# Selectors out of the identity, a new bank plan for the opening, and another order of loads in a fused attention and feed-forward kernel

## Chip, cores and metric

One NeuronCore of one Trainium2 chip. The metric is the device time of one execution in microseconds (us). A profile's span is about 1.8 us shorter than the time of its own run. Every run told here was at a mean granted TensorE clock of 0.99 to 1.0.

## The reference

The kernel takes float32 inputs: q, k, v of shape (8, 8, 576, 64), w_in (512, 2048), w_out (2048, 512). It gives (4608, 512) in float32. Cut to what matters:

```python
def phi(x):
    return np.where(x > 0, x, np.exp(x) - 1.0) + 1.0
q_p, k_p = phi(q), phi(k)
kv  = einsum('bhsd,bhse->bhde', k_p, v)
z   = sum(k_p, axis=2)
num = einsum('bhsd,bhde->bhse', q_p, kv)
den = einsum('bhsd,bhd->bhs', q_p, z)[..., None] + 1e-06
attn = num / den
x = attn.transpose(0, 2, 1, 3).reshape(4608, 512)
h = x @ w_in
out = (h - np.tanh(h)) @ w_out
```

## The kernel before

The feed-forward part is 9 chunks of 512 tokens, each of 64 dense 128x512 matmuls with w_in (16 column blocks `fi` by 4 pairs of heads `p`) and 64 with w_out. They run on TensorE one after the other. The attention of the 8 batches (576 tokens each) is threaded between them: lists `s1[fi]` and `s2[s]` say after which of the 16 w_in blocks, or after which of the 16 w_out steps, a piece of attention is put into the instruction streams. The kernel uses PSUM as one tile, `ps_all`, of eight banks of 128 x 512 float32.

To divide by the denominator, its reciprocal (it lies in four groups of 32 partitions, one for each quarter of the tokens, with a row per head) has to be spread over 128 partitions. Batches 0 and 1 do this on TensorE, by a matmul with a 0/1 matrix, the selector ("spread"), and then multiply on VectorE ("scale"). The later batches write the reciprocals to DRAM (`ds`) and read them back with a broadcast (`rdb`).

The parts that matter here; `...` marks a cut, the comments are mine, and the conditions on the chunk are worked out:

```python
s8 = const.tile([128, 3, NP, 2], F32, name="s8")
...
load_q(0)
make_identity(nc, ident)                  # POOL
load_k(0)
load_v(0)

nc.gpsimd.memset(s8, 0.0)                 # the selectors: 12 selects on POOL
for n in range(3):
    for t in range(4):
        r = slice(32 * t, 32 * t + 32)
        nc.gpsimd.affine_select(out=s8[r, n], in_=s8[r, n], compare_op=ALU.not_equal, fill=1.0,
            base=-8 * n, channel_multiplier=1, pattern=[[-1, NP], [-4, 2]])
for g in range(4):
    load_wi(g)                            # all loads are issued by POOL, in this order
load_k(1)
load_wo(0)
load_q(1)
load_wo(1)
load_v(1)
load_wo(2)
load_wo(3)
...
# opening: attention of batch 0
a_den(0, Banks([0]))
ns0 = new_ns(0)
b0_num(0, ns0, 1)                         # numerators in banks 4, 5; ACT copies them to ns0
b0_kv(1)
bp_a = a_spread_pe(0, 0, (0, 2))          # spread in banks 0 to 3
b0_kz(1)
b0_num(1, ns0, 6)
bp_b = a_spread_pe(0, 4, (1, 3))          # spread in banks 4 to 7
for n, p in enumerate((0, 2, 1, 3)):
    a_scale(0, p, ns0, (bp_a, bp_b)[n // 2], 144 * (n % 2))
...
# chunk 0: where the attention of batch 1 stands
s1[13].append(lambda: a_kphi(1, 0))
s1[15].append(lambda: a_kphi(1, 1))
s2[1].append(lambda: a_qphi(1, 0))
s2[3].append(lambda: a_qphi(1, 1))
s2[5].append(lambda: a_qT_pe(1, 0, side))
s2[6].append(lambda: a_qT_pe(1, 1, side))
s2[7].append(lambda: a_kv(1, side))
s2[9].append(lambda: (a_den(1, side), a_split(1)))
s2[10].append(num1)
s2[12].append(lambda: spread1(0))
s2[13].append(lambda: a_qphi(2, 0))
s2[14].append(lambda: spread1(1))
s2[15].append(lambda: (a_qphi(2, 1), a_qT_dma(2)))
...
# chunk 1: batch 2, and the loads of batch 3
s1[7].append(lambda: a_kv(2, attn))
s1[10].append(lambda: (a_den(2, attn), a_spread(2)))
for p in range(NP + 1):
    s2[9 + p].append(lambda p=p: a_num(2, p))
s1[1].append(lambda: a_kphi(2, 0))
s1[3].append(lambda: a_kphi(2, 1))
s1[0].append(lambda: (gate(gT, 0), load_k(3), load_q(3), load_v(3)))
```

## Time and profile before

| | |
|---|---|
| time, median of 3 runs | 303.54 us (303.45 to 303.79) |
| span of the profiled run (303.01 us) | 301.2 us |
| first product of k of batch 0 (opening) | 12.38 us |
| first w_in matmul of chunk 0 | 20.25 us |
| first w_out matmul of chunk 0 ("B") | 34.07 us |
| first w_in matmul of chunk 2 ("D") | 87.72 us |

The last four rows are starts on TensorE. From D to the end every kernel of this study takes 213.4 to 213.8 us, so a kernel is told by three lengths: the start of the first product of k, from there to B, and B to D. The page, the waits and the opening are shown in the prediction. One more view is worth having, the chain that ended last (start, us, what). In its first 40 us it goes, after k of batch 0, through two transfers of weights:

```profile
14.21 8.53 DMA w_in_sb<-in_moe_w_in_dram
23.03 15.81 DMA w_out_sb<-in_moe_w_out_dram
38.88 1.89 PE ps_all L333 x8
```

The second block of w_out arrives at 38.84 us, and the matmul that needs it starts at 38.88.

### The profile page before, as it was taken

What the parts mean: (1) busy time and instruction counts of PE and PEld (TensorE: products, weight loads), DVE (VectorE), ACT (ScalarE), POOL (GpSimd) and SP (SyncE); (2) the same over time, 40 slices, a digit from 0 to 9 for tenths busy, and PEclk for the clock granted to TensorE, in tenths of its full rate; (3) what the DMA queues carried; (4) which work ended last, traced back from release to release, by engine and by line L of the source; (5) the groups of instructions that cost most, each with busy time, mean ns of one, the idle gap of its engine ahead of it and who ended that gap; (6) DMA issues with size and microseconds to landing.
All of it is one profiled execution on the core that took longest, in us unless ns stands there. A gap on an engine that the chain in (4) does not pass through costs nothing.

```text
span 301.2 us, 4766 instructions
## 1 busy us (share of the span) xinstructions
PE 288.7 (96%) x1804; PEld 137.2 (46%) x1804; DVE 181.9 (60%) x313; ACT 149.6 (50%) x229; POOL 52.9 (18%) x100
## 2 busy tenths in 40 slices
PE   8869989899989999999999999999999999999994
PEld 2534454354445444544454445444544444444443
DVE  4779836898457854785578656865682458008600
ACT  3627824865625652566256625662562166127411
POOL 8963351060006000600060005100000000000000
PEclk9999999999999999999999999999999999999999
DMA  7899999988969776878788876977108310131032
GB/s 104 135 181 207 201 206 206 218 127 145 219 142 144 127 188 138 151 122 191 150 135 139 192 150 89 185 173 167 38 2 192 73 35 0 37 70 35 2 70 70
DMA packets 38902, 38.82 MB, mean 129 GB/s; under 512 B 16800, under 2 KB 33632, under 8 KB 38112
## 3 DMA queue, kind: packets, MB, share of 16 engines
q0 software_dynamic: 17600, 18.35, 38.2%
q1 hardware_dynamic: 21280, 20.17, 29.9%
q8 instruction: 14, 0.23, 0.3%
q14 instruction: 8, 0.07, 0.1%
HBM read 43.78 MB, written 9.55 MB: 177 GB/s over the span
## 4 chain that ended last, share of the span: by engine, by line
PE 79%; DMA 14%; DVE 2%; POOL 2%; ACT 1%; issue 1%; SPq 0%; DVEq 0%; ACTq 0%; POOLq 0%
PE ps_all L318 35%; PE ps_all L333 35%; DMA w_out_sb<-in_moe_w_out_dram 5%; PE ps_all L174 4%; DMA w_in_sb<-in_moe_w_in_dram 3%; DMA rdb<-ds 3%; PE ps_all L269 2%; DMA kraw<-in_k_dram 2%; DMA ds<-rden 1%; PE ps_all L515 1%; POOL qraw L88 1%; ACT e L131 1%; PE ps_all L226 1%; POOL kraw L88 1%; DVE xT L311 0%
## 5 line engine op out<-in xcount | busy, mean ns | idle before, releaser
L318 PE MATMUL ps_all<-xT,w_in_sb 128*128 128x512 bf16 x576 | 128.2, 379 | 2.4 <-DMA w_in_sb<-in_moe_w_in_dram 1.4
L333 PE MATMUL ps_all<-w_out_sb,gT 128*128 128x512 bf16 x560 | 128.3, 379 | 1.2 <-DMA w_out_sb<-in_moe_w_out_dram 1.2
L324 DVE TENSOR_TENSOR gT<-ps_all,th 128x512 bf16<-128x512 f32 x144 | 97.1, 688 | 51.0 <-ACT th L323 50.3
L323 ACT ACTIVATE th<-ps_all 128x512 f32<-128x512 f32 x144 | 85.2, 598 | 53.0 <-PE ps_all L318 48.0
L318 PEld LDWEIGHTS <-w_in_sb 128*128 128x128 bf16 x576 | 55.3, 98 | 69.5 <-issue 2.5
L333 PEld LDWEIGHTS <-gT 128*128 128x128 bf16 x560 | 54.0, 98 | 66.7 <-issue 3.3
L339 ACT COPY osb<-ps_all 128x512 f32<-128x512 f32 (+1 forms) x37 | 21.2, 574 | 78.4 <-PE ps_all L333 58.7
L280 DVE TENSOR_TENSOR xT<-ps_all,rdb 128x512 bf16<-128x512 f32 x24 | 16.3, 690 | 14.2 <-PE ps_all L269 12.1
L107 POOL DMA_DIRECT2D v<-in_v_dram x32 | 19.3, 644 | 8.5 <-DMA w_in_sb<-in_moe_w_in_dram 3.6
L131 ACT ACTIVATE e<-qraw 128x1152 bf16<-128x1152 bf16 x16 | 18.5, 1161 | 4.0 <-DMA qraw<-in_q_dram 4.0
L329 POOL COPY g<-gT 1x1 bf16<-1x1 bf16 x5 | 0.9, 177 | 109.7 <-DVE gT L324 109.7
L133 DVE TENSOR_TENSOR kp<-e,r 128x1152 bf16<-128x1152 bf16 x16 | 12.1, 758 | 12.1 <-ACT e L131 11.1
L131 ACT ACTIVATE e<-kraw 128x1152 bf16<-128x1152 bf16 x16 | 18.6, 1163 | 0.5 <-DMA kraw<-in_k_dram 0.5
L133 DVE TENSOR_TENSOR qp<-e,r 128x1152 bf16<-128x1152 bf16 x16 | 12.1, 758 | 8.1 <-ACT e L131 7.4
L174 PE MATMUL ps_all<-v,kp 64*128 64x192 bf16 x252 | 11.6, 243 | 0.0
L269 PE MATMUL ps_all<-qT,kz 128*128 128x512 bf16 x28 | 10.1, 379 | 1.4 <-DVE xT L280 1.4
L174 PEld LDWEIGHTS <-kp 64*128 64x128 bf16 x252 | 10.0, 94 | 3.0 <-issue 2.5
L390 PE MATMUL ps_all<-zero 128*128 128x512 bf16 x32 | 9.4, 455 | 1.2 <-DVE zero L346 1.2
L92 POOL DMA_DIRECT2D kraw<-in_k_dram x14 | 8.7, 635 | 6.6 <-ACT th L323 3.9
L92 POOL DMA_DIRECT2D qraw<-in_q_dram x14 | 8.8, 640 | 5.7 <-DVE qp L133 4.3
L132 DVE TENSOR_SCALAR r<-qraw 128x1152 bf16<-128x1152 bf16 x16 | 7.4, 464 | 2.3 <-DMA qraw<-in_q_dram 2.3
L183 DVE TENSOR_TENSOR kz<-ps_all,mask 128x320 bf16<-128x320 f32 x14 | 6.2, 485 | 3.4 <-PE ps_all L174 3.4
(72 smaller groups left out, 98.4 us busy)
## 6 DMA issues: line engine op xcount, KB each, us to landing
out_dram<-osb SPq DMA_DIRECT2D x70, 128.0 KB
rdb<-ds SPq DMA_DIRECT2D x12, 576.0 KB
v<-in_v_dram POOLq DMA_DIRECT2D x32, 144.0 KB, 7.9
kraw<-in_k_dram POOLq DMA_DIRECT2D x14, 288.0 KB, 5.0
qraw<-in_q_dram POOLq DMA_DIRECT2D x14, 288.0 KB, 7.3
w_in_sb<-in_moe_w_in_dram POOLq DMA_DIRECT2D x4, 512.0 KB, 9.5
w_out_sb<-in_moe_w_out_dram POOLq DMA_DIRECT2D x4, 512.0 KB, 13.7
qraw<-in_q_dram POOLq DMA_DIRECT2D x4, 144.0 KB, 3.8
```

What stands on the lines that cost most here:

```text
L92: nc.gpsimd.dma_start(out=t[64 * hg:64 * hg + 64].rearrange("p i h j d -> p (i h) (j d)"), in_=src[b, 4 * hg:4 * hg + 4].rearrange("h (p j ...
L107: nc.gpsimd.dma_start(out=v_b[b % 2][64 * hg:64 * hg + 64, i, 0:2].rearrange("p h j d -> p h (j d)"), in_=v[b, h0:h0 + 2].rearrange("h (p ...
L131: return (lambda: nc.scalar.activation(e, x, AF.Exp), lambda: nc.vector.tensor_scalar(r, x, 0.0, 1.0, ALU.max, ALU.add), lambda: nc.vector ...
L133: lambda: nc.vector.tensor_tensor(y, e, r, ALU.min))
L174: nc.tensor.matmul(ps[hg], kp[r, i, j].rearrange("p h d -> p (h d)"), vt[r, i, :, j, :], start=(j == 0), stop=(j == J - 1))
L269: nc.tensor.matmul(ps, kz[:, p // 2, p % 2, 0:128], qT[:, p % 2, 0:8, p // 2, :], start=True, stop=True)
L280: nc.vector.tensor_mul(xT[:, p, S * b:S * b + 512].rearrange("p (j t c) -> p j t c", j=8, t=4), ps.rearrange("p j (t c) -> p j t c", t=4), ...
L318: nc.tensor.matmul(h, w_in_sb[:, p, fi * 128:(fi + 1) * 128], xT[:, p, c * 512:(c + 1) * 512], start=(n == 0), stop=(n == NP - 1))
L323: nc.scalar.activation(th, h, AF.Tanh)
L324: nc.vector.tensor_sub(gT[:, fi, :], h, th)
L333: nc.tensor.matmul(o, gT[:, fi, i * 128:(i + 1) * 128], w_out_sb[:, fi, :], start=(fi == 0), stop=(fi == NF - 1))
L339: nc.scalar.copy(osb[:, f0:f1], o[:, f0:f1])
```

## The change

Its intent has four parts. (1) The selectors are cut out of the identity matrix by four small ACT copies and four DVE copies, so POOL issues w_in 4 us earlier. (2) The opening's spreads move to banks 4 to 7 so that w_in matmuls can start in banks 0 and 1 while the scales still run, with the last 64 tokens of batch 0 scaled by way of DRAM. (3) The second and third blocks of w_out are loaded ahead of q and v of batch 1. (4) The attention of chunks 0 and 1 is placed at other steps to fit. The core of the diff; `[...]` marks a cut, and the comments in added lines are mine:

```diff
-    s8 = const.tile([128, 3, NP, 2], F32, name="s8")
+    s8 = const.tile([128, 3, 2, NP], F32, name="s8")
[...]
-    nc.gpsimd.memset(s8, 0.0)
-    for n in range(3):
-        for t in range(4):
-            r = slice(32 * t, 32 * t + 32)
-            nc.gpsimd.affine_select(
-                out=s8[r, n], in_=s8[r, n], compare_op=ALU.not_equal, fill=1.0, base=-8 * n,
-                channel_multiplier=1, pattern=[[-1, NP], [-4, 2]])
     for g in range(4):
         load_wi(g)
     load_k(1)
     load_wo(0)
+    load_wo(1)
     load_q(1)
-    load_wo(1)
+    load_wo(2)
     load_v(1)
-    load_wo(2)
     load_wo(3)
[...]
+    for t in range(4):
+        nc.scalar.copy(s8[32 * t:32 * t + 32, 0].rearrange("q h p -> q (h p)"),
+                       ident[32 * t:32 * t + 32, 32 * t:32 * t + 8])
[...]
-    b0_num(0, ns0, 1)
+    b0_num(0, ns0)                 # now in banks 1 to 3
     b0_kv(1)
-    bp_a = a_spread_pe(0, 0, (0, 2))
     b0_kz(1)
-    b0_num(1, ns0, 6)
-    bp_b = a_spread_pe(0, 4, (1, 3))
-    for n, p in enumerate((0, 2, 1, 3)):
-        a_scale(0, p, ns0, (bp_a, bp_b)[n // 2], 144 * (n % 2))
+    b0_rest()                      # last 64 tokens: reciprocals to DRAM and back
+    b0_spread((0, 2), 0)           # banks 4 to 7, first 512 tokens
+    b0_scale(0, ns0, 0)
+    b0_scale(2, ns0, 1)
+    b0_num(1, ns0)
+    b0_spread((1, 3), 2)           # banks 4 to 7 again, other columns
+    b0_scale(1, ns0, 2)
+    b0_scale(3, ns0, 3)
[...]
-            s1[13].append(lambda: a_kphi(1, 0))
[...]
+            s1[6].append(lambda: b0_scale_rest(ns0))
+            s1[12].append(lambda: a_kphi(1, 0))
+            s1[14].append(lambda: a_kphi(1, 1))
+            s2[3].append(lambda: a_qphi(1, 0))
+            s2[5].append(lambda: a_qphi(1, 1))
+            s2[6].append(lambda: a_qT_pe(1, 0, side))
+            s2[7].append(lambda: a_qT_pe(1, 1, side))
+            s2[10].append(lambda: a_kv(1, side))
+            s2[12].append(lambda: (a_den(1, side), num1(), a_split(1)))
+            s2[14].append(lambda: spread1(0))
+            s2[15].append(lambda: (spread1(1), a_qphi(2, 0), a_qphi(2, 1), a_qT_dma(2)))
         elif n1 < B:
-            s1[7 if c == 1 else 5].append(lambda: a_kv(n1, attn))
-            s1[10 if c == 1 else 8].append(lambda: (a_den(n1, attn), a_spread(n1)))
+            s1[8 if c == 1 else 5].append(lambda: a_kv(n1, attn))
+            s1[11 if c == 1 else 8].append(lambda: (a_den(n1, attn), a_spread(n1)))
             for p in range(NP + 1):
-                s2[9 + p].append(lambda p=p: a_num(n1, p))
+                s2[(11 if c == 1 else 9) + p].append(lambda p=p: a_num(n1, p))
         if c == 1:
-            s1[1].append(lambda: a_kphi(2, 0))
-            s1[3].append(lambda: a_kphi(2, 1))
+            s1[4].append(lambda: a_kphi(2, 0))
+            s1[5].append(lambda: a_kphi(2, 1))
[...]
         if c == 0:
-            for n, p in enumerate((0, 2, 1, 3)):
-                for fi in range(4):
-                    l1mm(c, fi, hs[fi], p, n)
+            order = [(0, 0), (0, 1), (2, 0), (2, 1), (0, 2), (0, 3), (2, 2), (2, 3)]
+            order += [(p, fi) for p in (1, 3) for fi in range(4)]
+        elif c == 1:
+            hs = [dense() for fi in range(4)]
+            order = [(p, fi) for p in range(NP) for fi in range(4)]
[...]
```

In chunk 1 the first four blocks of w_in now go pair by pair, and their tanh, subtraction and attention pieces come after all sixteen matmuls. Cut from this excerpt is a small fifth piece: exp and minimum of the second half of k of batch 0 are done in two instructions each instead of one.

More of the change, by code (lines that the diff above doesn't have):

```diff
@@ L121, with phi_pieces @@
     kp_t, qp_t, qT_t, kz_t, rdb_t, rden_t = {}, {}, {}, {}, {}, {}
-    def phi_pieces(b, src, store, name, i):
+    def phi_pieces(b, src, store, name, i, parts=0):
         if i == 0:
@@ L130, in phi_pieces @@
         y = store[b][:, i].rearrange("p j h d -> p h j d")
+        if parts:
+            return ([lambda h=h: nc.scalar.activation(e[:, h], x[:, h], AF.Exp) for h in range(2)],
+                    lambda: nc.vector.tensor_scalar(r, x, 0.0, 1.0, ALU.max, ALU.add),
+                    [lambda h=h: nc.vector.tensor_tensor(y[:, h], e[:, h], r[:, h], ALU.min) for h in range(2)])
         return (lambda: nc.scalar.activation(e, x, AF.Exp),
@@ L206, in b0_kz, with b0_num @@
         nc.vector.tensor_mul(kz_t[0][:, :, i, 0:128], ps_all[:, 4 + 2 * i:6 + 2 * i, 0:128], mask[:, :, i, 0:128])
-    def b0_num(i, ns, rem):
+    def b0_num(i, ns):
         kz, qT = kz_t[0], qT_t[0]
         for hg in range(2):
-            nc.tensor.matmul(ps_all[:, rem, 64 * hg:64 * hg + 64], kz[:, hg, i, 0:128], qT[:, i, 8, hg, :],
+            nc.tensor.matmul(ps_all[:, 1, 64 * hg:64 * hg + 64], kz[:, hg, i, 0:128], qT[:, i, 8, hg, :],
                              start=True, stop=True)
@@ L214, in b0_num @@
         for hg in range(2):
-            nc.tensor.matmul(ps_all[:, 4 + hg, :].rearrange("p (j t) -> p j t", j=8), kz[:, hg, i, 0:128],
+            nc.tensor.matmul(ps_all[:, 2 + hg, :].rearrange("p (j t) -> p j t", j=8), kz[:, hg, i, 0:128],
                              qT[:, i, 0:8, hg, :], start=True, stop=True)
-        nc.scalar.copy(ns[:, i::2, 8, :], ps_all[:, rem, 0:128].rearrange("p (a t) -> p a t", a=2))
-        nc.scalar.copy(ns[:, i::2, 0:8, :].rearrange("p a j t -> p a (j t)"), ps_all[:, 4:6, :])
+        nc.scalar.copy(ns[:, i::2, 8, :], ps_all[:, 1, 0:128].rearrange("p (a t) -> p a t", a=2))
@@ new lines, in b0_num, with b0_spread, b0_scale @@
+        nc.scalar.copy(ns[:, i::2, 0:8, :].rearrange("p a j t -> p a (j t)"), ps_all[:, 2:4, :])
+    def b0_spread(pairs, n0):
+        for n, p in enumerate(pairs):
+            for t in range(4):
+                r = slice(32 * t, 32 * t + 32)
+                nc.tensor.matmul(ps_all[:, 4 + t, 128 * (n0 + n):128 * (n0 + n) + 128],
+                                 sel[r, p].rearrange("p h e -> p (h e)"), rden_t[0][r, 0:128], start=True, stop=True)
+    def b0_scale(p, ns, n):
+        nc.vector.tensor_mul(
+            xT[:, p, 0:512].rearrange("p (j t c) -> p t j c", j=8, t=4),
+            ns[:, p, 0:8].rearrange("p j (t c) -> p t j c", t=4),
+            ps_all[:, 4:8, 128 * n:128 * n + 128].rearrange("p t (j c) -> p t j c", c=16))
@@ new lines, in b0_rest @@
+    def b0_rest():
+        nc.vector.reciprocal(rden_t[0][:, 128:144], ps_all[:, 0, 128:144])
+        ds = dram.tile([H, 4, 16], F32, name="ds0")
+        for t in range(4):
+            nc.sync.dma_start(out=ds[:, t, :], in_=rden_t[0][32 * t:32 * t + H, 128:144])
+        rdb = rpool.tile([128, NP, 4, 16], F32, name="rdb0")
+        for hh in range(2):
+            nc.sync.dma_start(
+                out=rdb[64 * hh:64 * hh + 64].rearrange("p a t c -> p (a t c)"),
+                in_=ds[4 * hh:4 * hh + 4].rearrange("h t c -> (h t c)").partition_broadcast(64))
+        rdb_t[0] = rdb
@@ L220, in a_den, with b0_scale_rest @@
+    def b0_scale_rest(ns):
+        nc.vector.tensor_mul(
+            xT[:, :, 512:576].rearrange("p a (t c) -> p a t c", t=4),
+            ns[:, :, 8, :].rearrange("p a (t c) -> p a t c", t=4), rdb_t[0])
     def a_den(b, banks):
@@ L236, in a_den @@
         rden = rpool.tile([128, J * 16], F32, name="rden")
-        nc.vector.reciprocal(rden, den)
+        n = J * 16 if b > 0 else 128
+        nc.vector.reciprocal(rden[:, 0:n], den[:, 0:n])
         rden_t[b] = rden
@@ L305, in a_spread_pe @@
                 r = slice(32 * t, 32 * t + 32)
-                nc.tensor.matmul(bp[:, t, 144 * n:144 * n + 144], (sel3 if b else sel)[r, p].rearrange("p h e -> p (h e)"),
+                nc.tensor.matmul(bp[:, t, 144 * n:144 * n + 144], sel3[r, p].rearrange("p h e -> p (h e)"),
                                  rden_t[b][r], start=True, stop=True)
@@ L390, in spin @@
             nc.tensor.matmul(ps_all[:, 2, :], zero[:, 0:128], zero, start=True, stop=True)
+    for t in range(4):
+        nc.scalar.copy(s8[32 * t:32 * t + 32, 0].rearrange("q h p -> q (h p)"),
+                       ident[32 * t:32 * t + 32, 32 * t:32 * t + 8])
     side = Banks([4, 5, 6, 7])
@@ L398 @@
     a_qT_pe(0, 0, side, "AA")
-    (ek0, rk0, mk0), (ek1, rk1, mk1) = (phi_pieces(0, k_t, kp_t, "kp", i) for i in range(2))
+    (ek0, rk0, mk0), (ek1, rk1, mk1) = (phi_pieces(0, k_t, kp_t, "kp", i, 2 * i) for i in range(2))
     for f in (mq1, rk0, ek0):
@@ L403 @@
     a_qT_pe(0, 1, side, "VV")
-    for f in (ek1, rk1, mk0):
+    for f in (*ek1, rk1, mk0):
         f()
-    nc.scalar.copy(sel, s8[:, 0].unsqueeze(3).to_broadcast([128, NP, 2, 64]))
+    nc.scalar.copy(sel, s8[:, 0].rearrange("q h p -> q p h").unsqueeze(3).to_broadcast([128, NP, 2, 64]))
     spin(8)
     b0_z(0)
-    mk1()
+    for f in mk1:
+        f()
     b0_zc(0)
@@ L416 @@
     ns0 = new_ns(0)
-    b0_num(0, ns0, 1)
+    b0_num(0, ns0)
     b0_kv(1)
-    bp_a = a_spread_pe(0, 0, (0, 2))
     b0_kz(1)
-    b0_num(1, ns0, 6)
-    bp_b = a_spread_pe(0, 4, (1, 3))
-    for n, p in enumerate((0, 2, 1, 3)):
-        a_scale(0, p, ns0, (bp_a, bp_b)[n // 2], 144 * (n % 2))
+    b0_rest()
[6 more added lines that the diff above has]
+    b0_scale(3, ns0, 3)
     nc.vector.memset(v_b[1][:, :, 2], 1.0)
     nc.vector.memset(v_b[0][:, :, 2], 1.0)
-    s24 = rpool.tile([128, NP, 2], F32, name="s24")
-    nc.vector.tensor_add(s24, s8[:, 1], s8[:, 2])
-    nc.vector.tensor_reduce(part[:, 0:1], s24.rearrange("p a h -> p (a h)"), mybir.AxisListType.X, ALU.add, negate=True)
-    nc.vector.tensor_reduce(part[:, 1:2], s8[:, 2].rearrange("p a h -> p (a h)"), mybir.AxisListType.X, ALU.add, negate=True)
-    nc.vector.tensor_add(s24, s24, s8[:, 0])
-    nc.vector.tensor_copy(sel3, s24.unsqueeze(3).to_broadcast([128, NP, 2, 64]))
+    for t in range(4):
+        nc.vector.tensor_copy(s8[32 * t:32 * t + 32, 1:3].rearrange("q n h p -> q (n h p)"),
+                              ident[32 * t:32 * t + 32, 32 * t + 8:32 * t + 24])
+    s24 = rpool.tile([128, 2 * NP], F32, name="s24")
+    f8 = s8.rearrange("q n h p -> q n (h p)")
+    nc.vector.tensor_add(s24, f8[:, 1], f8[:, 2])
+    nc.vector.tensor_reduce(part[:, 0:1], s24, mybir.AxisListType.X, ALU.add, negate=True)
+    nc.vector.tensor_reduce(part[:, 1:2], f8[:, 2], mybir.AxisListType.X, ALU.add, negate=True)
+    nc.vector.tensor_add(s24, s24, f8[:, 0])
+    nc.vector.tensor_copy(
+        sel3, s24.rearrange("q (h p) -> q p h", h=2).unsqueeze(3).to_broadcast([128, NP, 2, 64]))
     load_q(2)
@@ L455, in num1 @@
                     a_num_copy(1, sub["ns"], p, side)
-            s1[13].append(lambda: a_kphi(1, 0))
-            s1[15].append(lambda: a_kphi(1, 1))
-            s2[1].append(lambda: a_qphi(1, 0))
-            s2[3].append(lambda: a_qphi(1, 1))
-            s2[5].append(lambda: a_qT_pe(1, 0, side))
-            s2[6].append(lambda: a_qT_pe(1, 1, side))
-            s2[7].append(lambda: a_kv(1, side))
-            s2[9].append(lambda: (a_den(1, side), a_split(1)))
-            s2[10].append(num1)
-            s2[12].append(lambda: spread1(0))
-            s2[13].append(lambda: a_qphi(2, 0))
-            s2[14].append(lambda: spread1(1))
-            s2[15].append(lambda: (a_qphi(2, 1), a_qT_dma(2)))
+            s1[6].append(lambda: b0_scale_rest(ns0))
[9 more added lines that the diff above has]
+            s2[15].append(lambda: (spread1(1), a_qphi(2, 0), a_qphi(2, 1), a_qT_dma(2)))
         elif n1 < B:
-            s1[7 if c == 1 else 5].append(lambda: a_kv(n1, attn))
-            s1[10 if c == 1 else 8].append(lambda: (a_den(n1, attn), a_spread(n1)))
+            s1[8 if c == 1 else 5].append(lambda: a_kv(n1, attn))
+            s1[11 if c == 1 else 8].append(lambda: (a_den(n1, attn), a_spread(n1)))
             for p in range(NP + 1):
-                s2[9 + p].append(lambda p=p: a_num(n1, p))
+                s2[(11 if c == 1 else 9) + p].append(lambda p=p: a_num(n1, p))
         if c == 1:
-            s1[1].append(lambda: a_kphi(2, 0))
-            s1[3].append(lambda: a_kphi(2, 1))
+            s1[4].append(lambda: a_kphi(2, 0))
+            s1[5].append(lambda: a_kphi(2, 1))
         if c >= 1 and n2 < B:
@@ L486 @@
         if c == 0:
+            first = Banks([4, 5, 6, 7, 0, 1, 2, 3])
             hs = [ps_all[:, fi, :] for fi in range(4)]
-            first = Banks([4, 5, 6, 7, 0, 1, 2, 3])
-            for n, p in enumerate((0, 2, 1, 3)):
-                for fi in range(4):
-                    l1mm(c, fi, hs[fi], p, n)
+            order = [(0, 0), (0, 1), (2, 0), (2, 1), (0, 2), (0, 3), (2, 2), (2, 3)]
[3 more added lines that the diff above has]
+            order = [(p, fi) for p in range(NP) for fi in range(4)]
+        if c < 2:
+            seen = [0] * 4
+            for p, fi in order:
+                l1mm(c, fi, hs[fi], p, seen[fi])
+                seen[fi] += 1
             for fi in range(4):
                 l1act(fi, hs[fi], gT)
-        for fi in range(4 if c == 0 else 0, NF):
+            for fi in range(4):
+                for f in s1[fi]:
+                    f()
+        for fi in range(4 if c < 2 else 0, NF):
             h = first() if c == 0 else dense()
```

## The prediction

> **What bounds the kernel now.** I read the page first, then the sums of waits, then the timeline of the first 90 us, and last busy time and DMA traffic us by us. The page:
>
> ```profile
> span 301.2 us, 4766 instructions
> PE 288.7 (96%) x1804; PEld 137.2 (46%) x1804; DVE 181.9 (60%) x313; ACT 149.6 (50%) x229; POOL 52.9 (18%) x100
> PEclk9999999999999999999999999999999999999999
> PE 79%; DMA 14%; DVE 2%; POOL 2%; ACT 1%; issue 1%; SPq 0%; DVEq 0%; ACTq 0%; POOLq 0%
> ```
>
> TensorE is busy for 288.7 of 301.2 us at full clock, so the 1136 dense 128x512 matmuls (64 take 13.8 us in the chain, 0.216 us each) set the time; about 12.5 us can be won at most. The change touches no steady-state matmul. What counts is when TensorE stands still. Of the waits, these are TensorE's in the stretch that the diff touches (engine, what it did next, what it waited for, us in total, times, longest):
>
> ```profile
> PE ps_all L318 <- DMA w_in_sb<-in_moe_w_in_dram: 1.4, 1, 1.4
> PE ps_all L269 <- DVE xT L280: 1.4, 1, 1.4
> PE ps_all L333 <- DMA w_out_sb<-in_moe_w_out_dram: 1.2, 1, 1.2
> PE ps_all L306 <- ACT ns L218: 1.1, 1, 1.1
> PE ps_all L318 <- DVE xT L311: 1.0, 2, 0.7
> ```
>
> After 90 us, us-by-us busy time shows TensorE full in every window up to the last output, so only the opening, chunk 0 and chunk 1 can change. The opening in the timeline (start, us, engine, operation):
>
> ```profile
> 8.95 0.22 POOL L354 MEMSET s<- 128x24 f32 x1
> 9.25 4.22 POOL L358 TENSOR_SCALAR_AFFINE_SELECT s<-s 32x8 f32<-32x8 f32 x12
> 13.43 3.03 POOL L113 DMA_DIRECT2D w_in_sb<-in_moe_w_in_dram  x4
> 15.59 0.77 PE L306 MATMUL ps_all<-rden,sel 32*128 32x144 f32 x16
> 15.61 0.43 DVE L206 TENSOR_TENSOR kz<-ps_all,mask 128x256 bf16<-128x256 f32 x1 [0.16 <-PE ps_all L202]
> 16.49 1.42 DVE L311 TENSOR_TENSOR xT<-ns,ps_all 128x576 bf16<-128x576 f32 x2 [0.46 <-PE ps_all L306]
> 18.06 0.77 PE L306 MATMUL ps_all<-rden,sel 32*128 32x144 f32 x16 [1.10 <-ACT ns L218]
> 20.25 13.99 PE L318 MATMUL ps_all<-xT,w_in_sb 128*128 128x512 bf16 x64 [1.41 <-DMA w_in_sb<-in_moe_w_in_dram]
> ```
>
> POOL spends 8.95 to 13.43 us on selectors before it issues w_in, and the first dense matmul starts at 20.25 us, when the first quarter of w_in has landed, although TensorE was free at 18.83. Meanwhile the DMA runs dry (columns: stretch, us, busy us of PE, PEld, DVE, ACT, POOL, then clock, DMA share, GB/s):
>
> ```profile
> 12.00:13.00 1.00, 0.62 (x32) 0.62 (x34) 0.92 (x2) 0.88 (x2) 0.95 (x2) 1.00 1.15 192
> 14.00:15.00 1.00, 1.00 (x22) 0.46 (x24) 0.61 (x1) 0.30 (x2) 1.00 (x3) 1.00 0.11 25
> 18.00:19.00 1.00, 0.77 (x16) 0.56 (x16) 0.03 (x1) 0.01 (x1) 1.00 (x2) 1.00 1.25 202
> ```
>
> From 16 to 53 us it moves about 205 GB/s throughout: a transfer bound, in which the order of issue decides what lands when.
>
> **What the Trainium skill says.** "DMA: Bandwidth & Descriptors", section "Issuing engines are not separate DMA queues": transfers from all engines share the same 16 DMA engines and interleave. So an earlier w_in helps only while these have nothing to do; the trace has such a hole (25 GB/s at 14 us). "Perfetto Trace Analysis", section "Per-instruction lifecycle: what the profiler-reported window actually captures": the slice of a GpSimd-issued DMA ends with descriptor generation, not with the data. The trace agrees: an issue takes 0.78 us, the landing came 6.8 us after the first. "PSUM — Partial Sum Buffer", section "PSUM bank collisions raise a hardware error": two engines must not be in one bank and quadrant at once, even at different columns; guard by bank. The trace fits it: the first scale starts at 16.49, after all 16 spread matmuls, not after the eight of its own pair. It matters, because the new plan puts both spreads into banks 4 to 7.
>
> **The change, part by part.**
>
> Selectors: 12 selects and a memset, 4.48 us of POOL, go. Four small ACT copies out of the identity take their place. The identity is ready at 4.33 and ACT waits for q until 5.78; the smallest ACT copy in this trace (128x1) takes 0.20 us, so 0.8 us fits in. w_in is issued from about 9.1 us. It still queues behind v of batch 0, whose bytes flow until 13.2. Working by bytes: 1.73 MB had moved by 13.0; the first quarter needs 1.77 + 0.52 MB plus about 0.25 MB that the trace has in flight ahead of a landing (k landed at 11.10 with 1.36 MB moved for 1.18 MB). That is 0.75 MB more at 205 GB/s: landing near 16.7, 3.6 earlier. All later weights move by the same.
>
> Bank plan: the first spread moves behind the kz product of the second half, which ends at 16.04 and frees banks 6 and 7: the two of its eight products that go to banks 4 and 5 pass before, the rest ends near 16.75. Two scales, now 512 wide (0.747 x 512/576 = 0.66 us), end at 18.15. The second spread needs the same banks, hence 18.2 to 18.9, where before it waited for ACT until 18.06. The first dense matmuls need only xT 0 and 2, w_in and banks 0 and 1: they start at about 18.75. The last two scales (19.0 to 20.3) are ready when eight dense matmuls are done (20.5). **Gain 1.5 us, not 3.6:** the wait for w_in becomes one for PSUM and DVE.
>
> Last tokens by DRAM: four writes of 16 columns and two broadcasts. In chunk 1 the like path took 4.8 us (69.43 to 74.20) and 8.6 us (74.3 to 82.86), with nine times the bytes. From 16.3 I expect a landing at 25 to 28. Its consumer stands in DVE's order behind fi 6, at about 28, because 3 us of memsets and selector work come first. Eight banks of slack lie under it: 0 us.
>
> w_out ahead of q and v: in order of bytes the second quarter lands 3.6 + 2.9 (0.59 MB of q no longer ahead) earlier than 38.84, near 32.3; it is wanted at 18.75 + 13.8 + 3.45 = 36.0. The whole hole goes, from the sixteenth matmul's slot at 37.52 to 38.88: **gain 1.36 us**. q lands near 35.3; exp and min (1.16 + 0.76) give 37.4, wanted at 38.6. v of batch 1 near 40.8, wanted at 43. Tight, 0 us.
>
> End of chunk 0: den, num and split are now at one step and the spreads one step apart instead of two. With t0 the end of den on TensorE, w is ready at t0 + 2.9 (add 0.31, reciprocal 1.05, split 1.2, gaps), the four ns copies on ACT at about t0 + 2.9; TensorE arrives at t0 + 2.8: 0.15 lost. The second spread waits until the first two scales (1.42 us) have released the banks: 0.8 lost. In return the p-outer order of chunk 1 takes away the two waits for xT (0.69 + 0.29). **Sum 0.**
>
> Start of chunk 1: both q phis of batch 2 stand ahead of the subtractions, and four subtractions plus fi 4 ahead of the first k phi. Counted from the second spread's end, DVE has 1.42 (scales) + 2.46 (q; 1.23 a phi as at 36.2 to 38.7) + 5 x 0.625 (subtractions back to back) + 1.23 = 8.2 us to the first half of kp, another 1.85 to the second. TensorE comes to kv after 36 matmuls, at 7.8. It waits about 0.7, works 0.8 on the first half, waits 1.0 again. Before, the kv wait was under 0.1. **Loss 1.7 us.**
>
> Numerators of chunk 1: den one step later, the products two steps later. From den's end to the third product TensorE has 18 x 0.863 + 0.44 = 16.0 us of work, before 15.1; the chain by DRAM took 16.6. **Gain 0.9 us** of the wait of 1.41.
>
> Sum: 303.54 - 1.5 - 1.36 + 1.7 - 0.9 = 301.5, or 301.4 with the smaller ends rounded in my favour.
>
> **Rivals.** (a) The DVE debt of chunk 1 does not appear, because TensorE's own small waits or a quicker drain cover it: then 1.5 + 1.4 + 0.9, possibly 1.0 at the chunk's border, and 299 to 299.7. For it: ACT and DVE are only 50% and 60% busy. Against: at this border before, DVE runs from 54.57 to 62.29 nearly without a break, and kv began only 0.1 us after it. (b) w_in is what sets the start as before, and all of its 3.6 us arrives, with the spreads not held by bank: start at 17.0 to 18.0 and 300.5. Against: the scales end at 18.15 by DVE's durations. (c) DMA order bites: q or v of batch 1 or the DRAM round trip is late behind w_out, and ACT and then TensorE stall: 302.5 to 304. For it: the DMA is full until 53 us and q's margin is 1.2 us. Against: everything starts 3.6 us earlier.
>
> **Range and chances.** Each of the four terms is uncertain by about 0.7 us, their root sum 1.4, with somewhat more room below: 299.4 to 302.8. Faster by over 2% needs 297.5 or less, that is every hole of 5.1 us gone, kv wait absent and more: 0.04. Slower by over 2% needs 309.6: 0.01. Within 2%: 0.95.
>
> **What would show it.** w_in's issue near 9.1 and its first landing near 16.7; first dense matmul at 18.5 to 19, waiting for the spread or the scale and not for w_in; no hole before the second quarter of w_out; waits of 0.5 to 1 us for the second spread of batch 1; two waits for kp in kv of batch 2, 1.7 us together; a wait under 0.8 us before the third product of batch 2; TensorE full after that. I am wrong if the first dense matmul comes before 18.0 or still waits for w_in, or if kv of batch 2 does not wait.

## The result, and the profile after

| | before | after |
|---|---|---|
| time, median (range) | 303.5 (303.24 to 303.79), 4 runs | 301.56 (301.34 to 302.27), 4 runs |
| ratio of fast runs, 95% interval | | 0.994 (0.9921 to 0.9959) |
| span of the profiled run | 301.2 | 299.9 |
| first product of k | 12.38 | 12.71 |
| first w_in matmul of chunk 0 | 20.25 | 19.24 |
| from the first product of k to B | 21.69 | 20.36 |
| B to D | 53.65 | 53.18 |

A ratio is the mean time of one kernel's fast runs over that of the other's fast runs of the same rounds, so it is not quite the ratio of the medians quoted. The result is 0.6% faster: inside the range, and within 2%. The changed kernel's page:

```profile
span 299.9 us, 4765 instructions
PE 288.8 (96%) x1804; PEld 137.4 (46%) x1804; DVE 181.9 (61%) x320; ACT 150.2 (50%) x234; POOL 48.7 (16%) x87
PE 83%; DMA 6%; DVE 6%; POOL 2%; issue 1%; ACT 1%; SPq 0%; DVEq 0%; POOLq 0%; ACTq 0%
```

TensorE is busy for as long as before (288.8 against 288.7 us). POOL has lost 4.2 us and 13 instructions. The chain that ended last has 6% of DMA in it instead of 14%, and 6% of DVE instead of 2%: TensorE now waits for VectorE. The four of its waits in the first 100 us that matter here, by the same columns as before:

```profile
PE ps_all L307 <- DVE xT L318: 1.2, 1, 1.2
PE ps_all L179 <- DVE kp L138: 1.2, 2, 0.9
PE ps_all L230 <- DVE xT L234: 0.9, 1, 0.9
PE ps_all L344 <- DVE xT L349: 0.6, 1, 0.6
```

Both waits for weights are gone. In their place stand the second spread of the opening (L230), the second spread of batch 1 (L344) and kv of batch 2 (L179); the third numerator product of batch 2 (L307) still waits. The opening in the timeline:

```profile
4.36 0.81 ACT L424 CAST s<-ident 32x8 f32<-32x8 bf16 x4 [2.13 <-POOL ident masks.py:199]
9.28 3.17 POOL L113 DMA_DIRECT2D w_in_sb<-in_moe_w_in_dram  x4 [0.24 <-DMA kraw<-in_k_dram]
15.82 1.31 PE L230 MATMUL ps_all<-rden,sel 32*128 32x128 f32 x16
17.24 1.29 DVE L234 TENSOR_TENSOR xT<-ns,ps_all 128x512 bf16<-128x512 f32 x2 [0.72 <-PE ps_all L230]
18.58 0.73 PE L230 MATMUL ps_all<-rden,sel 32*128 32x128 f32 x16 [0.86 <-DVE xT L234]
19.24 13.99 PE L356 MATMUL ps_all<-xT,w_in_sb 128*128 128x512 bf16 x64
```

w_in is issued 4.15 us earlier (9.28 against 13.43), but the first w_in matmul starts only 1.0 us earlier. It no longer waits for w_in: it stands behind the second spread, which waits 0.86 us until DVE has read the first. The hole in the transfers at 14 us is filled (DMA share and GB/s are the last two columns):

```profile
14.00:15.00 1.00, 0.79 (x24) 0.35 (x16) 0.52 (x3) 0.14 (x1) 1.00 (x2) 1.00 1.24 207
```

Between B and D only 0.47 us is won. In chunk 1, kv of batch 2 ran without a break before, and now stops twice (this is TensorE's timeline, before and then after):

```profile
62.38 1.66 PE L174 MATMUL ps_all<-v,kp 64*128 64x192 bf16 x36
83.72 0.38 PE L269 MATMUL ps_all<-qT,kz 128*128 128x512 bf16 x1 [1.41 <-DVE xT L280]
```

```profile
60.85 0.92 PE L179 MATMUL ps_all<-v,kp 64*128 64x192 bf16 x18 [0.33 <-DVE kp L138]
62.68 0.92 PE L179 MATMUL ps_all<-v,kp 64*128 64x192 bf16 x18 [0.91 <-DVE kp L138]
83.98 0.38 PE L307 MATMUL ps_all<-qT,kz 128*128 128x512 bf16 x1 [1.25 <-DVE xT L318]
```

The wait for the third product became 1.25 us, hardly less than 1.41, though the product was moved two steps later to do away with it. (Over more profiles the gain is larger; see the section on the prediction.)

### The profile page after: what moved, and what is told of

Same layout as the page of the kernel before. It is cut to its first block, busy times and chain, and to the rows that moved or that the text cites. A ratio compares the mean times of both kernels' runs of the same rounds, so it can differ in the third digit from the quotient of the medians.

```text
span 299.9 us, 4765 instructions
## 1 busy us (share of the span) xinstructions
PE 288.8 (96%) x1804; PEld 137.4 (46%) x1804; DVE 181.9 (61%) x320; ACT 150.2 (50%) x234; POOL 48.7 (16%) x87
## 3 DMA queue, kind: packets, MB, share of 16 engines
q0 software_dynamic: 17600, 18.35, 38.2%
## 4 chain that ended last, share of the span: by engine, by line
PE 83%; DMA 6%; DVE 6%; POOL 2%; issue 1%; ACT 1%; SPq 0%; DVEq 0%; POOLq 0%; ACTq 0%
PE ps_all L356 38%; PE ps_all L371 35%; PE ps_all L179 3%; DMA rdb<-ds 3%; DMA kraw<-in_k_dram 2%; PE ps_all L307 2%; DMA ds<-rden 2%; PE ps_all L566 1%; DVE gT L362 1%; PE ps_all L263 1%; POOL qraw L88 1%; DVE kp L138 1%; DVE xT L349 1%; DVE rden L275 1%; POOL kraw L88 1%
## 5 line engine op out<-in xcount | busy, mean ns | idle before, releaser
L138 DVE TENSOR_TENSOR kp<-e,r 128x1152 bf16<-128x1152 bf16 x15 | 11.4, 757 | 12.0 <-ACT e L136 11.1
L136 ACT ACTIVATE e<-kraw 128x1152 bf16<-128x1152 bf16 x15 | 17.4, 1161 | 0.0
L179 PE MATMUL ps_all<-v,kp 64*128 64x192 bf16 x252 | 11.8, 243 | 1.2 <-DVE kp L138 1.2
L179 PEld LDWEIGHTS <-kp 64*128 64x128 bf16 x252 | 10.0, 94 | 4.5 <-issue 2.5
L307 PE MATMUL ps_all<-qT,kz 128*128 128x512 bf16 x28 | 10.1, 379 | 1.2 <-DVE xT L318 1.2
## 6 DMA issues: line engine op xcount, KB each, us to landing
w_out_sb<-in_moe_w_out_dram POOLq DMA_DIRECT2D x4, 512.0 KB, 16.6
```

Of the source, the lines that this page charges most:

```text
L136: return (lambda: nc.scalar.activation(e, x, AF.Exp), lambda: nc.vector.tensor_scalar(r, x, 0.0, 1.0, ALU.max, ALU.add), lambda: nc.vector ...
L138: lambda: nc.vector.tensor_tensor(y, e, r, ALU.min))
L179: nc.tensor.matmul(ps[hg], kp[r, i, j].rearrange("p h d -> p (h d)"), vt[r, i, :, j, :], start=(j == 0), stop=(j == J - 1))
L307: nc.tensor.matmul(ps, kz[:, p // 2, p % 2, 0:128], qT[:, p % 2, 0:8, p // 2, :], start=True, stop=True)
```

## The experiments

Twelve runs followed, in three groups of four; two of them repeat a kernel. The kernels of a group shared one chip and the runs of the kernel before, and the three groups were on three chips; compare medians within a group. All gave correct results. "Ratio" is against the kernel before of the same rounds, with a 95% interval.

| run | median (range), us | kernel before, us | ratio | first product of k | to B | B to D |
|---|---|---|---|---|---|---|
| *group 1* | | | | | | |
| e1_sel_only | 300.78 (300.54–301.12) | 302.85 | 0.993 (0.989–0.996) | 12.56 | 20.21 | 52.52 |
| e2_order_only | 303.49 (303.19–306.48) | 302.85 | 1.004 (1.000–1.008) | 13.24 | 20.39 | 54.33 |
| e3_old_sched | 302.10 (301.62–302.25) | 302.85 | 0.997 (0.994–1.000) | 13.08 | 20.36 | 53.35 |
| e4_kphi_mid | 300.34 (299.94–300.46) | 302.85 | 0.991 (0.988–0.994) | 13.06 | 20.36 | 51.62 |
| *group 2* | | | | | | |
| after_again | 301.86 (301.67–301.96) | 303.11 | 0.995 (0.993–0.997) | 13.10 | 20.36 | 52.93 |
| e1_again | 300.89 (300.72–301.06) | 303.11 | 0.992 (0.990–0.994) | 12.92 | 20.21 | 52.33 |
| e5_v3_late | 300.25 (300.06–300.74) | 303.11 | 0.990 (0.988–0.992) | 12.72 | 20.36 | 51.78 |
| e6_all | 298.94 (298.69–299.09) | 303.11 | 0.985 (0.983–0.988) | 12.66 | 19.92 | 50.88 |
| *group 3* | | | | | | |
| e7_no_sel | 303.98 (303.31–304.71) | 302.96 | 1.004 (1.002–1.006) | 13.11 | 20.50 | 54.53 |
| e8_old_open | 301.43 (300.63–302.61) | 302.96 | 0.995 (0.993–0.997) | 12.82 | 20.21 | 53.02 |
| e9_old_order | 302.42 (301.71–303.67) | 302.96 | 0.999 (0.997–1.001) | 13.03 | 20.86 | 52.98 |
| e10_best | 298.37 (297.95–299.81) | 302.96 | 0.986 (0.983–0.988) | 12.68 | 19.92 | 50.36 |

The last three columns are lengths in us from the profiled run. The first of them scatters between 12.38 and 13.24 with the landing of q and k of batch 0, ahead of anything that the change touches; that is why one profiled run against another can mislead by 0.8 us.

### e1_sel_only and e1_again: the selectors alone

The kernel before, with nothing but the selectors taken out of the identity:

```diff
-    nc.gpsimd.memset(s8, 0.0)
-    [the 12 selects]
+    for t in range(4):
+        nc.scalar.copy(s8[32 * t:32 * t + 32, 0]..., ident[32 * t:32 * t + 32, 32 * t:32 * t + 8])
[... and four DVE copies for the other two thirds, layouts to match]
```

> The kernel before with the selectors alone taken out of the identity; bank plan, order of loads and schedule as before. My theory: w_in is issued near 9.3 us and its first quarter lands near 17.1, so TensorE starts the dense work when it comes free, near 18.9 (1.4 earlier); the second quarter of w_out lands about 2.5 earlier, near 36.3, just as it is wanted, so the 1.4 us hole shrinks under 0.3; the waits for xT (1.0) and for the DRAM trip in chunk 1 (1.4) stay. Sum about -2.5: 301.0 us, as good as the whole change or better. Rival: the loads are bound by bytes, so the hole of w_out returns in full or the DRAM trip's end stays where it was, and only about 1 us is left: 302.5.

Measured: 300.78 us, 2.07 below the kernel before of the same rounds. To have it beside the whole change on one chip, it ran again:

> The changed kernel unaltered, as the control of these rounds: 0.993 to 0.995 of the kernel before, about 301.5 us, and the same waits within 0.3 us (second spread 0.9, kp in kv 1.2, third product of batch 2 1.2).

> The selectors alone once more, now beside the changed kernel. If the first run told the truth, it is as fast as the whole change or up to 0.8 us faster: 300.7 to 301.5. Rival (the gap between the two was the other chip's): 0.5 us or more slower than the changed kernel of these rounds.

Measured: 300.89 for the selectors alone, 301.86 for the whole change; the ranges do not touch. One part in four gives the whole gain, and the other three together cost about 1 us. By the starts: B comes at 32.77, 33.13 and 33.03 us in the three profiles with the old opening and the selectors off POOL (e1, e1_again, e8), and at 34.07, 33.63 and 33.61 in the three with them on POOL (before, e2, e7), on the mean 0.8 us apart; and B to D falls from 53.65 to 52.52 and 52.33, that is by 1.2. The two make the 2.0 us. The profile of e1_again shows why the new bank plan had little to win (TensorE's timeline):

```profile
18.60 0.77 PE L306 MATMUL ps_all<-rden,sel 32*128 32x144 f32 x16 [1.10 <-ACT ns L218]
19.30 1.04 PE L318 MATMUL ps_all<-xT,w_in_sb 128*128 128x512 bf16 x3
```

(The x3 is where this view ends, at 20 us.) With w_in early, the first w_in matmul of the old opening, too, stands right behind the second spread. That spread waits 1.10 us for ACT; in the new plan it waits 0.86 us for DVE. The hole before the second block of w_out is gone as well, without any new order of loads: w_out moved up with w_in.

### e2_order_only: the order of loads alone

The kernel before with the new order:

```diff
     load_wo(0)
+    load_wo(1)
     load_q(1)
-    load_wo(1)
+    load_wo(2)
     load_v(1)
-    load_wo(2)
     load_wo(3)
```

> The kernel before with the order of loads alone changed (w_out ahead of q and v of batch 1). My theory: the hole of 1.4 us before the second quarter of w_out closes, but q of batch 1 lands near 38.9 instead of 36.3 and the old schedule wants its transposes near 39.3; with 1.9 us for exp and min TensorE waits about 1.5 us there instead: 303.2 to 303.6, no gain. Rival: q is in time and the hole is simply gone: 302.2.

Measured: 303.49, ratio 1.004, no gain. The timelines of ACT and TensorE:

```profile
38.50 2.22 ACT L131 ACTIVATE e<-qraw 128x1152 bf16<-128x1152 bf16 x2 [2.73 <-DMA qraw<-in_q_dram]
40.51 0.68 PE L161 MATMUL ps_all<-ident,qp 128*128 128x128 bf16 x9 [1.54 <-DVE qp L133]
```

The wait for w_out is gone, and ACT now waits 2.73 us for q of batch 1, which costs TensorE 1.54 us at the transposes of q. In a stretch where the DMA is full, the order only chose who waits.

### e3_old_sched: the changed kernel with the old placing of the attention

```diff
-            s1[12].append(lambda: a_kphi(1, 0))
-            [... the new steps of chunks 0 and 1, and chunk 1 pair by pair]
+            s1[13].append(lambda: a_kphi(1, 0))
+            [... the old steps; b0_scale_rest stays]
```

> The changed kernel with the schedule of chunks 0 and 1 of the kernel before (opening, order of loads and the DRAM trip of the last tokens stay). My theory: the new schedule of chunks 0 and 1 is worth about nothing in sum, because what it gains at the border (1.0 for xT) it loses in kv of batch 2 (1.5): 301.3 to 302.0, with a wait for xT of about 1.0 and no wait for kp in kv; a stall of up to 1 us for q or v of batch 1, which now stand behind w_out, would add to that. Rival: the schedule carries the gain: 303 or more.

Measured: 302.10. B to D is 53.35, against 53.18 and 52.93 in the two profiles of the changed kernel. The waits are others: 1.0 us for xT at the start of chunk 1, 1.5 before the third product, none in kv, and one for q of batch 1 at its transposes (TensorE's timeline):

```profile
39.54 0.68 PE L166 MATMUL ps_all<-ident,qp 128*128 128x128 bf16 x9 [0.76 <-DVE qp L138]
```

Their sum is nearly the same. Under the new order of loads the new placing is worth some 0.2 to 0.4 us by the profiles; the changed kernel did not run in this group, so the times can't be compared.

### e4_kphi_mid: phi of k of batch 2 earlier in chunk 1

In the changed kernel, the two phis of k stand behind the second and third subtraction of chunk 1, not behind the fifth and sixth:

```diff
             for fi in range(4):
                 l1act(fi, hs[fi], gT)
+                if c == 1 and fi in (1, 2):
+                    a_kphi(2, fi - 1)
[... and out of s1[4] and s1[5]]
```

> The changed kernel with the k phis of batch 2 moved between the first four tanh and subtractions of chunk 1. Both theories: the wait of TensorE for kp in kv (1.5 us) falls under 0.3. Theory A (DVE debt and the DRAM trip set the end): the debt comes back at den, the reciprocal ends at most 0.3 earlier than 68.95, rdb lands when it did, and the wait before the third product grows by what kv gave: 301.3, gain 0.2. Theory B (the kv wait itself lies on the path): 300.1, gain 1.4.

Measured: 300.34. B to D is 51.62, 1.3 to 1.6 us less than in the two profiles of the changed kernel, which did not run in this group: theory B's gain. kv of batch 2 runs without a wait, as expected. The reciprocal starts only 0.27 us earlier (67.63 against 67.90), also as expected. What I had not expected is that the third product starts 1.2 us earlier all the same. The timelines of POOL, the SP queue and TensorE, first of the changed kernel (its third product is shown above), then of e4:

```profile
62.29 1.23 POOL L92 DMA_DIRECT2D kraw<-in_k_dram  x2 [4.88 <-ACT th L361]
68.98 1.28 SPq L295 DMA_DIRECT2D ds<-rden  x4
74.73 1.12 SPq L298 DMA_DIRECT2D rdb<-ds  x2
```

```profile
60.87 1.23 POOL L92 DMA_DIRECT2D kraw<-in_k_dram  x2 [3.09 <-ACT th L361]
68.71 1.30 SPq L295 DMA_DIRECT2D ds<-rden  x4
73.67 1.12 SPq L298 DMA_DIRECT2D rdb<-ds  x2
82.77 0.38 PE L307 MATMUL ps_all<-qT,kz 128*128 128x512 bf16 x1 [0.90 <-DVE xT L318]
```

The loads of batch 3 go into the buffers of k and q that the phis have read, so earlier phis release them 1.42 us earlier. The small writes to `ds` are issued only 0.27 us earlier, yet the read-back can start 1.06 us earlier: its time follows the loads, not the reciprocal. (B came 0.35 us later in e4 than in the profile it is compared with. Counted from B the loads move by 1.77 us, the writes by 0.62 and the read-back by 1.41, which says the same.) That made a new theory: the loads of batch 3 hold up the round trip.

### e5_v3_late: v of batch 3 out of the way

In the changed kernel, v of batch 3 is loaded only after the first product of batch 2:

```diff
+            if c == 1:
+                s2[12].append(lambda: (gate_x(2), load_v(3)))
[...]
-            s1[0].append(lambda: (gate(gT, 0), load_k(n2), load_q(n2), load_v(n2)))
+            s1[0].append(lambda: (gate(gT, 0), load_k(n2), load_q(n2)))
+            if c > 1:
+                s1[0].append(lambda: load_v(n2))
```

`gate_x` is a POOL copy of one element of xT, which makes POOL wait for that product's scale.

> The changed kernel, but v of batch 3 is loaded after the first product of batch 2 and not right behind k and q. Theory C: the first half of the DRAM trip (reciprocals to DRAM) lands only when the loads of batch 3 are through (73.6 us, when traffic falls from 205 GB/s), so without 0.59 MB of v it lands about 2.5 us earlier, rdb lands near 81 instead of 83.1, and the wait of 1.25 us before the third product is gone: 1.0 to 1.3 us faster than the changed kernel. Rival: the trip is latency of its own, the wait stays within 0.3 us: no gain.

Measured: 300.25 against 301.86 in the same group, and no wait before the third product. The SP queue's timeline:

```profile
69.00 1.35 SPq L295 DMA_DIRECT2D ds<-rden  x4
73.36 1.12 SPq L298 DMA_DIRECT2D rdb<-ds  x2
```

From the end of the four `ds` issues to the issue of the read-back (start of `rdb` less start and length of `ds`) it takes:

| | us |
|---|---|
| before | 74.36 - 70.79 = 3.57 |
| changed kernel | 74.73 - 70.26 = 4.47 |
| changed kernel, again | 75.00 - 70.67 = 4.33 |
| e4_kphi_mid (k, q, v 1.42 us earlier) | 73.67 - 70.01 = 3.66 |
| e5_v3_late (v away) | 73.36 - 70.35 = 3.01 |
| e6_all (both) | 70.33 - 69.26 = 1.07 |

The bytes of `ds` are the same in all six. The theory stands against its rival, with a smaller size: I had expected the first half of the trip to end 2.5 us earlier, and the read-back was issued 1.4 to 1.6 us earlier than in the two profiles of the changed kernel. By the landing times in the fourteen traces, the read-back is issued between 1.2 us before and 0.9 us after the last load of batch 3 issued ahead of it has landed. Why such small writes take so long beside the loads, the runs do not show.

### e6_all: the three repairs together

e4 and e5, and in the opening two w_in matmuls ahead of the second spread, so that TensorE works while DVE reads the first:

```diff
     b0_num(1, ns0)
+    for fi in range(2):
+        l1mm(0, fi, ps_all[:, fi, :], 0, 0)
     b0_spread((1, 3), 2)
[... and these two out of the order of chunk 0]
```

> The changed kernel with three repairs: k phis of batch 2 between the first four subtractions, v of batch 3 late, and two dense matmuls of pair 0 ahead of the second spread of the opening, which waits for DVE to leave banks 4 to 7. If the three holes lie one behind the other in the path of TensorE, they add up: 1.5 (kp) + 0.9 to 1.2 (third product) + 0.4 (spread): 298.6 to 299.0 us, 0.985 of the kernel before. Rival: one of them was covered by another and the gain is 1.5 or less: 300.0.

Measured: 298.94, ratio 0.985, 2.92 us below the changed kernel on the same chip. The gains add up for the most part: against after_again the way to B is 0.44 us shorter and B to D 2.05 us, where e4 and e5 alone had 1.31 and 1.15. That is 0.4 us short of their sum; the wait for the third product, which both shorten, explains only 0.1 of it (0.99 to 0.90 us in e4), and the rest stays open. The SP queue's timeline shows the round trip with v of batch 3 out of its way and q all but landed (69.90 us):

```profile
67.97 1.29 SPq L295 DMA_DIRECT2D ds<-rden  x4
70.33 1.12 SPq L298 DMA_DIRECT2D rdb<-ds  x2
```

The 0.44 us ahead of B show that the changed opening stood still at a border of its own making, and two matmuls that need neither the second spread nor its banks fill part of that. With them the new opening is 0.3 us shorter than the old one with early w_in (19.92 against 20.21).

### e7_no_sel: the changed kernel with its selectors back on POOL

```diff
+    nc.gpsimd.memset(s8, 0.0)
+    [the 12 selects, in the new layout]
[... the copies out of ident taken away]
```

> The changed kernel with its selectors built on POOL again, everything else of the change kept. If the selectors are what the change lives on, w_in is issued near 13.4 again, dense work starts at 19.8 to 20.3, q of batch 1 lands near 39 and is waited for by about 1 us: 302.8 to 303.5, no faster than the kernel before. Rival: bank plan, order and schedule carry a gain of their own: under 302.4.

Measured: 303.98, ratio 1.004 (1.002 to 1.006): slower than the kernel before, and 0.5 us more than I had expected. ACT and TensorE in the timeline:

```profile
39.42 2.22 ACT L136 ACTIVATE e<-qraw 128x1152 bf16<-128x1152 bf16 x2 [3.48 <-DMA qraw<-in_q_dram]
41.43 0.68 PE L166 MATMUL ps_all<-ident,qp 128*128 128x128 bf16 x9 [1.60 <-DVE qp L138]
```

It is the wait of e2 again. The new order of loads can be afforded only because the selectors left POOL: in the changed kernel ACT waits 0.85 us for q, and that is hidden; without the earlier issue it is 3.48 us. Together with e1 this settles that the gain of the whole change is the selectors'. Not tried: to leave the selects on POOL, but behind the issue of w_in.

### e8_old_open: the changed kernel with the old opening

Old banks, spreads 144 columns wide, no trip by DRAM for the last tokens:

```diff
-    b0_rest()
-    b0_spread((0, 2), 0)
-    [...]
+    bp_a = a_spread_pe(0, 0, (0, 2))
     b0_kz(1)
+    b0_num(1, ns0, 6)
+    bp_b = a_spread_pe(0, 4, (1, 3))
[... and the four scales of before]
```

> The changed kernel with numerators, spreads and scales of batch 0 as in the kernel before (144 wide, old banks, no DRAM trip for the last tokens). From the first product of k of batch 0 to the first product of w_out the old plan took 20.21 us with free selectors, the new one 20.36: so 0.1 to 0.2 us faster than the changed kernel, within the noise of these rounds (301.4 to 301.9). Rival: the new bank plan is worth a gain and this is 0.5 us or more slower.

Measured: 301.43, ratio 0.995, the same as the changed kernel's in the other two sets. The way to B is 20.21 in all three profiles with the old opening and early w_in (e1, e1_again, e8), and 20.36 in those of the new one (after, after_again, e3, e4, e5). The new bank plan costs 0.15 us; it wins nothing.

### e9_old_order: the changed kernel with the old order of loads

```diff
     load_wo(0)
-    load_wo(1)
     load_q(1)
-    load_wo(2)
+    load_wo(1)
     load_v(1)
+    load_wo(2)
     load_wo(3)
```

> The changed kernel with the old order of loads (q ahead of the second quarter of w_out, v ahead of the third). With the selectors gone the second quarter lands about 2.5 us earlier than in the kernel before, near 36.3, and is wanted near 36.5: a hole of 0 to 0.3 us, so the order is worth nothing any more: 301.6 to 302.1. Rival: the hole of 1.4 us comes back: 303.

Measured: 302.42, some 0.3 to 0.8 us worse than I had expected. The profile does not explain it by the order: the wait for w_out is 0.19 us, and B to D (52.98) is as in the changed kernel. Its way to B is 0.5 us longer, of which 0.31 is a wait for v of batch 0, which was issued before the orders differ. Whether the other executions had the same I can't tell from one profile. So what the order is worth in the changed kernel stays open between 0.2 us, by the trace, and about 1 us, by the times.

Beside e1 and e3 its profile does show where the other parts lose. With the selectors off POOL, B to D is:

| | old placing | new placing |
|---|---|---|
| old order | 52.52, 52.33 (e1, e1_again) | 52.98 (e9) |
| new order | 53.35 (e3) | 53.18, 52.93, 53.02 (changed kernel twice, e8) |

To the old placing the new order adds 0.9 us, of which 0.76 is e3's wait for q; to the old order the new placing adds 0.6, with the two waits in kv; both together add 0.6. These are single profiles, e3 and e9 with the new opening, which lies ahead of B.

### e10_best: e6 with the end of batch 1 one step earlier

```diff
-            s2[10].append(lambda: a_kv(1, side))
-            s2[12].append(lambda: (a_den(1, side), num1(), a_split(1)))
-            s2[14].append(lambda: spread1(0))
+            s2[9].append(lambda: a_kv(1, side))
+            s2[11].append(lambda: (a_den(1, side), num1(), a_split(1)))
+            s2[13].append(lambda: spread1(0))
```

> The three repairs together (k phis between the first subtractions, v of batch 3 late, two dense matmuls ahead of the second spread) and the border of chunk 0 spaced as before: kv, den and the first spread of batch 1 one step earlier, so that the second spread comes two steps after the first. The wait of 0.8 us for the second spread should go: 298.0 to 298.3 us, 0.982 to 0.984 of the kernel before. Rival: v of batch 1 is late for the earlier kv, or DVE's debt fills the place: 298.9.

Measured: 298.37, ratio 0.986. The wait of 0.6 us for the second spread of batch 1 is gone from the profile, and B to D is 0.52 us shorter than in e6. The ratio is that of e6 (0.9858 against 0.9854, on another chip), so in time a gain over e6 is not shown. Either is about 1.4% faster than the kernel before and about 1% faster than the changed one.

## Why the prediction was right, and where it was not

The time was right: 301.4 predicted, 301.56 measured, nothing above 2%. Of the five terms two were the right size and three were too large:

| term | predicted | measured (profiles before and after) |
|---|---|---|
| opening | -1.5 | -1.0, start of the first w_in matmul |
| hole before the second block of w_out | -1.36 | gone, as predicted (the list of waits gave it 1.2) |
| end of chunk 0 | 0 | 0: 0.18 and 0.80 in (50.44 - 48.44 - 1.82 and 52.34 - 50.67 - 0.87, starts less the undisturbed steps of e1), 0.69 and 0.29 out |
| kv of batch 2 | +1.7 | +1.24 idle (0.33 and 0.91) |
| third product of batch 2 | -0.9 | -0.16 (1.41 to 1.25); -0.42 in the second profile; -0.55 on the mean of five profiles each |
| sum | -2.06 | -1.47 by the start of D, not by adding the rows; -1.94 in the medians |

- **Selectors.** The issue of w_in came at 9.28 (said: 9.1), the four ACT copies took 0.81 us (said: 0.8) and were hidden. The first quarter had landed by 17.20, when POOL, which waited for it, went on (said: 16.7). The prediction's sum has a slip: its terms, 1.77 + 0.52 + 0.25 - 1.73, make 0.81 MB and not 0.75, which gives 16.95; by the trace the landing was at 16.92. The later quarters came 2.7 us earlier, not 3.6.
- **Opening.** The mechanism was right: the wait for w_in became one for PSUM and DVE. The second spread went into the same banks as the first, at other columns, and waited 0.86 us for the first pair of scales to end: guarded by bank, as the prediction took from the Trainium skill ("PSUM — Partial Sum Buffer", section "PSUM bank collisions raise a hardware error"). The start was 19.24, where I had worked out 18.75. I had added up TensorE's work and the scales but not the 0.3 us by which this run's attention began later (12.71 against 12.38); counted from the first product of k the gain to B is 1.33. What I did not see is that the old opening would have had the same gain (e1, e8), since its own second spread would have waited for ACT at the same place. The gain belongs to the selectors; the bank plan as it was changed loses 0.15. Nor is the wait for w_in of the kernel before a fixed 1.4 us: in the profiles of e2 and e7, with the selectors on POOL, w_in matmuls started at 19.80 and 19.65 without it.
- **Last tokens by DRAM.** The read-back was issued at 22.00, the scale ran at 29.16 and nothing waited for it, as said.
- **w_out ahead of q and v.** The hole vanished, but e1 shows that it vanishes with the selectors alone, and e2 and e7 that the order by itself gives its gain back at q. I named that margin (1.2 us) as rival (c) and held it to be enough because "everything starts 3.6 us earlier". That is the point: the order lives on the selectors' gain and adds little of its own. The second block of w_out landed at 33.60, q at 36.39 and v at 41.82, each 1.0 to 1.3 us later than said by the trace's landing times, and still in time for TensorE.
- **kv of batch 2.** Right in kind, with two waits; e4 shows that it was the DVE's debt of subtractions ahead of the phis. Even DVE's 8.2 us to the first half of kp came true (52.57 to 60.80). The size has a slip: 8.2 less 7.8 is a first wait of 0.4 us, not the 0.7 written, and 0.33 was measured; the second was 0.91, not 1.0.
- **Third product of batch 2: the step that failed.** The prediction said: "From den's end to the third product TensorE has 18 x 0.863 + 0.44 = 16.0 us of work, before 15.1; the chain by DRAM took 16.6." It took the chain's length as fixed. TensorE's side came true (16.1 us, from 66.65 to 82.73), but the chain took 17.3 us, to 83.98. In the runs its length is not fixed; its end moves with the loads of batch 3. The reciprocal came 0.45 us earlier than before, the loads were issued 0.33 us later (62.29 against 61.96, since the phis that release their buffers had been moved back), and the read-back was issued 0.37 us later. e4 and e5 show it from both sides. So moving phi of k back cost twice: at kv, and at the end of a round trip 20 us on. One pair of profiles makes the miss too large, though: the wait is 1.24 to 1.73 us, on the mean 1.51, in the five profiles with the old placing (before, e1, e1_again, e2, e3), and 0.68 to 1.25, on the mean 0.96, in five with the new one (after, after_again, e7, e8, e9). About 0.55 of the 0.9 us was gained.

That the total came out right is therefore partly luck: two gains were taken 0.2 to 0.7 us too large each, and kv's loss 0.5 too large. Rivals (a), no debt in chunk 1, and (b), the whole of w_in's earlier arrival, did not come; (c) came in e2 and e7, where the selectors stay on POOL.

## What to carry to other kernels

Before judging a change of four parts, run its smallest part alone: here a short edit that takes 4.5 us of work off the engine that issues the loads was worth 2 us, and the three cleverer parts gave 1 us of it back. In a stretch where the DMA is full, a new order of loads may only move a wait, as in e2, e3 and e7, so look at who is next in line. The small round trip by DRAM ended here at about the time when the bulk loads issued before it were through: its length was not a constant to plan with, and holding back a load that nobody needed yet repaired it.

## What the Trainium skill lacked or had wrong

- "DMA: Bandwidth & Descriptors", section "Latency and other measured facts", puts the least DRAM round trip at about 0.8 us and the access latency at 2 us at high load. Where the bulk loads were nearly through, the trace comes near the former (from the end of the last `ds` issue to the issue of the read-back 1.07 us in e6 and 1.53 in e10). Beside bulk loads the same four writes of 4.5 KB took 3.0 to 4.5 us. The page says in "Queues, rings and completion order" that a DMA engine takes turns between queues packet by packet, but has no duration for a small transfer of one queue beside bulk loads of another. Here TensorE's wait behind it was 0.7 to 1.7 us.
- The same page, section "Bandwidth", has its measured rates for transfers of 4 KB to 16 MB, and no page has one for transfers that cast on the way. Here q, k, v and the weights are cast from float32 to bf16 by the load, and the traces before and after show about 205 GB/s from 16 to about 50 us, in either order. The queue's 18.35 MB is the bf16 size of the inputs, so these are bytes written; the float32 bytes read are twice as many.
- No page says what a small select on GpSimd costs: twelve of 32x8 elements took 4.22 us, 0.35 us each, nearly half of what the issue of a load takes there (0.78 us). ACT copied such blocks in 0.20 us each (four in 0.81).
